# Sequence transform of batches 2 to 7: four 32-row tiles in two rounds, in place of two 63-row tiles in one stretch

## Chip, core and metric

The kernel runs on one core of a Trainium2 chip. The metric is the device time of one execution in microseconds (us); the time of a kernel is the median of its runs.

## What is computed

```python
X = np.fft.fft(x, axis=1)          # x: 8 batches x 3008 points x 256 features, f32
X = np.fft.fft(X, axis=2).real     # only the real part is kept
t = X.reshape(24064, 256)
gate = 1 / (1 + np.exp(-(t @ w_gate)))     # w_gate, w_val: 256 x 1536
out = (gate * (t @ w_val)) @ w_out         # w_out: 1536 x 256
```

## The kernel before

The transform along the features is multiplied into the gate and value weights once, at the start (`merge`, L331 and L332). What is left for each batch is a cosine and a sine transform along the 3008 points, and the gated network on its results.

**Steps.** The main loop has 576 steps, 72 for each batch (`per`): six chunks of 252 (the last 246) frequencies times twelve 128-wide tiles of the 1536 hidden features. Step i issues on TensorE (PE), in this order: `front_a` (two products into PSUM tile `pf`, from `pk`, the cosine transform), `back` (five products of hidden tiles `h` and their sums `sf` with the output weights `wf`, into the five PSUM banks `po0` to `po4`, for hidden tiles that are five steps older), and `front_b` (two products into `pf` from `qk`, the sine transform). Every f32 product is two weight loads and two matmuls in the trace. ScalarE (ACT) takes, in each step, a sigmoid (L658), a doubled copy of `pf` (`part`, L644), two writes that start the `pf` of the next step (`seed`, L629) and a second sigmoid (L672). `front_b(i)` adds into `pf` and so waits for `part(i)`. VectorE (DVE) takes three gate operations per step (L659, L671, L675; L675 waits for the second sigmoid), and two or three from the list `later` (sums and transposes of finished chunks, L765 and L773). GpSimd (POOL) forms the sums `sf` (L681), seven in one step of three and six in another; `back` reads them in the third to fifth step after.

**Transform of the next batch.** During the 72 steps of one batch the next one is prepared. DMAs on SyncE's queue (SP) write a mirrored copy of its input into DRAM (`mirror_x`, L157 to L166) and load it (`load_x`, L147) into the one buffer `x4`. POOL folds it there in 24 operations (`fold_ops`, L405 to L443), DVE adds six turns (`turn`, L454). At step 40 of the 72, right behind `front_b`, `whole` runs the four groups (block 0 or 1; cosine or sine) in one stretch on PE: per group 12 products of 63 or 62 rows, even rows of the input into PSUM tile `ev` with partitions 0 to 63, odd rows into `od` with partitions 64 to 127, each with 189 or 188 columns of the tables in tile `st`. ACT copies (L512, L518) and 16 DVE operations (L514, L524, L528) put them together into the `pk` and `qk` of the next batch. The tables for batches 1 to 7 are made once, during batch 0 (`table_again`, `table_odd`, L212 to L225).

The order of all engines is written by hand: each engine executes its instructions in the order in which the program issues them. `at(i, f)` puts `f` at the end of step i:

```python
def at(i, *fs):
    side.setdefault(i, []).extend(fs)
```

Of the kernel before, what the change touches and what calls it, by code (L numbers as in the profile page):

```python
# [12 lines left out]
ALU = mybir.AluOpType  # L13
# [68 lines left out]
def kernel(  # L82
# [50 lines left out]
    def mm(o, l, r, start, stop):  # L133
        nc.tensor.matmul(o, l, r, start=start, stop=stop, skip_group_check=True)  # L134
# [13 lines left out]

    XR = {}

    def mirror_x(b):


        copy = nc.sync.dma_start
        src = xf[b]
        dst = XR[b] = dram.tile([P, 4, NQ, D], F32, name=f"xr{b}")
        ops = [lambda: copy(out=dst[HP - 2 : HP, :, NQ - 1],  # L157
                            in_=zero[:, :, 0:D].to_broadcast([2, 4, D]))]

        def rows(par):  # L160
            copy(out=dst[par * HP : (par + 1) * HP, :, 0:N3], in_=src[0:HP, :, par:NQ:2])

        def mirror(par, q):
            t = M // 2 - 2 * q - par
            lo, p0, n = par * HP, t // NQ, HP - 2 * ((par, q) == (0, N3 - 1))
            copy(out=dst[lo : lo + n, :, N3 + q].rearrange("p h d -> h p d"),  # L166
                 in_=src[p0 - n + 1 : p0 + 1, :, t % NQ].rearrange("p h d -> h p d")[:, ::-1])
        for par in range(2):
            ops.append(lambda par=par: rows(par))
            ops += [lambda par=par, q=q: mirror(par, q) for q in range(N3)]  # L170
        return ops
# [59 lines left out]
        return tangent, lambda: inner(0), lambda: half(0), lambda: inner(1), lambda: half(1), ends  # L231

    assert NPR == 6
    jobs = [(0, 0), (1, 0), (0, 1), (1, 1), (2, 0), (0, 2), (1, 2), (2, 1), (0, 3), (1, 3), (0, 4), (1, 4),
# [157 lines left out]

    W = {}
    TURN = {}

    def fold_ops(b, nq):
        x4 = X.pop(b)
        if not b:  # L400
            x4 = x4[0:NP]
        ops = []

        def point(e, i, j, q):
            e.tensor_tensor(x4[:, i, q, 1:D], x4[:, i, q, 1:D], x4[:, j, q, D - 1 : 0 : -1],  # L405
                            op=ALU.add)

        def first(e, i, j, q):
            e.tensor_tensor(x4[:, i, q, 0], x4[:, i, q, 0], x4[:, j, q, 0], op=ALU.add)

        def feat(e, v, r, q):
            e.memset(r[:, q, 0:1], 0.0)
            e.tensor_tensor(r[:, q, 1:HD], v[:, q, 1:HD], v[:, q, D - 1 : HD : -1],
                            op=ALU.subtract)
            e.tensor_tensor(v[:, q, 1:HD], v[:, q, 1:HD], v[:, q, D - 1 : HD : -1], op=ALU.add)

        def across(e, blk, q):
            e.tensor_tensor(x4[:, 1 - blk, q], x4[:, 0, q], x4[:, 2, q],  # L418
                            op=(ALU.add, ALU.subtract)[blk])

        parts = [(x4[:, 1], x4[:, 3]), (x4[:, 0], x4[:, 2])]
        qs = [slice(q, q + nq) for q in range(0, NQ, nq)]
        pool = nc.gpsimd
        if b == 1:

            for i in (0, 2):
                ops.append(lambda i=i: first(pool, i, i + 1, slice(0, NQ)))
            for q in qs:
                ops += [lambda i=i, q=q: point(pool, i, i + 1, q) for i in (0, 2)]
            for q in qs:  # L430
                ops += [lambda blk=blk, q=q, e=pool if q is qs[-1] else nc.vector: across(e, blk, q) for blk in range(2)]
        elif b:

            for i in (0, 2):
                ops += [lambda i=i, q=q: point(pool, i, i + 1, q) for q in qs]
                ops.append(lambda i=i: first(pool, i, i + 1, slice(0, NQ)))
            for blk in range(2):
                ops += [lambda blk=blk, q=q: across(pool, blk, q) for q in qs]
        if b:
            ops += [lambda q=q: feat(pool, *parts[1], q) for q in qs]  # L440
            for i, op in enumerate((ALU.add, ALU.subtract)):
                for ds in (slice(0, HD), slice(HD, D)):
                    ops.append(lambda i=i, op=op, ds=ds: pool.tensor_tensor(  # L443
                        x4[:, 3, i * N3 : (i + 1) * N3, ds], x4[:, 1, 0:N3, ds],
                        x4[:, 1, N3:, ds], op=op))
            parts[0] = x4[:, 3], x4[:, 1]
            slots = x4.rearrange("p i q d -> p (i q) d")

            def turn(q, minus):

                y = [slots[:, q : q + 16 : 15], slots[:, q + N3 : q + N3 + 10 : 9]]
                if minus:
                    y.reverse()
                nc.vector.scalar_tensor_tensor(  # L454
                    out=y[0][:, :, HD:D], in0=y[1][:, :, 0:HD], scalar=(ST[3], ST[4])[minus][:, q : q + 1],
                    in1=y[0][:, :, 0:HD], op0=ALU.mult, op1=ALU.add)
            TURN[b] = [lambda q=q, minus=minus: turn(q, minus) for q in range(N3) for minus in range(2)]
            ops += [lambda q=q: feat(pool, *parts[0], q) for q in qs]
        else:

            def half_rows(q):
                even, odd = slice(0, 4, 2), slice(1, 4, 2)
                point(nc.vector, even, odd, q)
                first(nc.vector, even, odd, q)
                for blk in range(2):
                    across(nc.vector, blk, q)
                v, r = x4[:, 0:2, q], x4[:, 2:4, q]
                for to, op in ((r, ALU.subtract), (v, ALU.add)):
                    nc.vector.tensor_tensor(to[:, :, :, 1:HD], v[:, :, :, 1:HD], v[:, :, :, D - 1 : HD : -1],  # L469
                                            op=op)  # L470
                nc.vector.memset(r[:, :, :, 0:1], 0.0)
            ops += [lambda q=q: half_rows(q) for q in qs]
        for blk, (v, r) in enumerate(parts):
            if b and blk:
                W[b, blk] = v[:, :, HD:D], r[:, :, HD:D]
                continue
            W[b, blk] = v[:, :, 0:HD], r[:, :, 0:HD], v[:, :, HD : HD + 1]
        return ops
# [52 lines left out]
    def whole(b, blk, what):  # L531
        _, then, both = seq_group(b, blk, what, (2, 3) if what else (0, 1))
        both()
        return then()

    def seq_start(b):
        PQE[b] = [pqp.tile([P, NK + 1], F32, name=name, tag=name) for name in ("pk", "qk")]
# [331 lines left out]
    e_rows(0)  # L869

    per = NFT * len(chunks)
    side = {}

    def at(i, *fs):
        side.setdefault(i, []).extend(fs)
# [34 lines left out]
    for i in range(i0, count, i0):  # L910
        at(i - (8 if i == i0 else 11), lambda i=i: e_rows(i))

    for b in range(B - 1):
        s0 = b * per
        g0 = s0 + 3 * i0 + 4 if b else 5 * i0 + 4


        slots = [i for i in range(s0 - 2 * i0 if b > 1 else s0 if b else 2 * i0, g0 - 2)
                 if i % i0 < (4 if b > 1 else 6)]

        def folds(slots, b=b):
            ops = fold_ops(b + 1, 2)
            for i, f in enumerate(ops):
                at(slots[i * len(slots) // len(ops)], f)
            for i, f in enumerate(TURN.pop(b + 1)):
                at(58 + i if b == 0 else slots[-1] - 1 + i * 4 // 6, f)
        if b == 0:

            slots = [20, 20, 20, 21, 21, 22, 23, 24, 24, 25, 26, 27, 27, 29, 31, 33, 35, 37, 39, 41, 43, 50, 53, 55]
            assert len(slots) == 24  # L930
        at(slots[0] - 1, lambda slots=slots, folds=folds: folds(slots))
        at(g0 - 2, lambda b=b: seq_start(b + 1))
        for blk in (1, 0):
            at(g0, *[lambda b=b, blk=blk, what=what: whole(b + 1, blk, what)() for what in range(2)])
        if b < B - 2:
            at(g0 + 1, lambda b=b: load_x(b + 2))
            for i, f in zip(calm(s0 if b else 3 * i0), mirror_x(b + 2)):
                at(i, f)

    at((B - 2) * per + 4 * i0 + 8, lambda: [at((B - 2) * per + 4 * i0 + 9 + 2 * i, f) for i, f in enumerate(plain_ops())])  # L940

    for i in range(count):
        if i != 1:
            front_a(i)
        if i == 0:
            front_a(1)
        if i:
            gate_a(i - 1)
        part(i)
        if i == 0:  # L950
            weight_parts(5)
        if N1 <= i + 1 < count:
            seed(i + 1)
        if i:
            gate_b(i - 1, *join.pop(i, []))
        for f in pre.pop(i, []) + out_use.pop(i, []):
            f()
        if i >= 5:
            back((i - 5) // 3, (i - 5) % 3)
        merges = use.pop(i, [])  # L960
        for f in merges[0 : min(i, 1)]:
            f()
        front_b(i)
        for f in merges[min(i, 1) :]:
            f()
        n = 3 if i >= count - 8 else 2 + (i % 2 and i not in (3 * i0 + 7, 3 * i0 + 9))
        for f in later[0:n]:
            f()
        del later[0:n]
        for f in side.pop(i, []):  # L970
            f()
# [55 lines left out]
```

## Time and profile before

| | |
|---|---|
| runs | 1923.06, 1923.21, 1923.45 us; median 1923.21 |
| span of the profiled execution, from first to last instruction | 1921.4 us; its whole time is not shown apart, the runs' median is 1.8 us more than the span |
| granted TensorE clock | 1.000 |
| busy: PE / DVE / ACT / POOL | 99% / 74% / 70% / 79% |
| one step in the steady state | 3.125 us of PE, from one `front_a` to the next |
| steps 78, 83 and 84 begin at | 305.1, 320.7 and 323.9 us |
| steps 113 and 125 begin at | 423.0 and 460.6 us |

How to read it: a line of a table of groups gives the source line, the engine, the operation, what it writes and reads with shapes and count, then busy time and the mean of one, then the engine's idle time just before them and who ended it. A timeline row gives start and length; rows of the same instruction are merged ("x2"). "63*128" is rows times columns of the weights of a matmul.

### The profile page before, as it was taken

To read this page: it belongs to the slowest core of one execution; us is meant where nothing else is said; L and a number is where in the kernel's file an instruction comes from. 1 tells how busy PE (TensorE), PEld (TensorE's weight loads), DVE (VectorE), ACT (ScalarE), POOL (GpSimd) and SP (SyncE) were. 2 spreads that over 40 slices of the span, in tenths; PEclk is the share of its full clock that TensorE was granted. 3 is DMA by queue.
4 is the path that set the end of the run, shared out by engine and by line. 5 is a ranking of instruction groups with operands and counts; after the bars stand their busy time and mean duration, and the time that the engine had idled before them with its cause. 6 is when DMAs were issued, how large, how long until landed. Compare 5 with 4: busy or idle time off the path is not lost.

```text
span 1921.4 us, 34211 instructions
## 1 busy us (share of the span) xinstructions
PE 1910.5 (99%) x11164; PEld 1776.2 (92%) x11164; DVE 1429.4 (74%) x3225; ACT 1344.2 (70%) x3148; POOL 1524.8 (79%) x2733
## 2 busy tenths in 40 slices
PE   8999999999999999999999999999999999999999
PEld 5789999999999999999999999999999999999998
DVE  7677877787777777778677777777777687777775
ACT  4876767767777677776777767777677767777775
POOL 2489969978898788987888878888788977877770
PEclk9999999999999999999999999999999999999999
DMA  8353222120131211202111121121200100011011
GB/s 313 110 98 78 66 80 60 48 80 15 22 78 23 80 20 41 61 14 82 26 47 48 20 84 19 47 52 23 80 15 15 27 15 15 14 21 21 15 16 31
DMA packets 173633, 97.02 MB, mean 50 GB/s; under 512 B 134429, under 2 KB 164360, under 8 KB 171664
## 3 DMA queue, kind: packets, MB, share of 16 engines
q1 hardware_dynamic: 172878, 94.32, 20.2%
q8 instruction: 90, 1.47, 0.3%
q14 instruction: 87, 0.71, 0.1%
q10 hardware_dynamic: 546, 0.51, 0.1%
q0 software_dynamic: 32, 0.00, 0.0%
HBM read 70.08 MB, written 46.71 MB: 61 GB/s over the span
## 4 chain that ended last, share of the span: by engine, by line
PE 98%; DMA 1%; DVE 1%; ACT 0%; issue 0%; SPq 0%; ACTq 0%
PE pf L134 51%; PE po L134 43%; PE ev L134 3%; DMA x<-in_xf_dram 1%; PE od L134 1%; PE ps L134 1%; DMA raw<-in_moe_w_val_dram 0%; PE pe L134 0%; DVE z L659 0%; DVE wf L307 0%; ACT wl L389 0%; DVE x L418 0%; DVE x L469 0%; DVE x L405 0%; ACT ae L644 0%
## 5 line engine op out<-in xcount | busy, mean ns | idle before, releaser
L681 POOL TENSOR_TENSOR sf<-h 128x168 f32<-128x168 f32 (+1 forms) x920 | 511.0, 575 | 215.5 <-DVE h L675 215.2
L681 POOL TENSOR_TENSOR sf<-h,sf 128x168 f32<-128x168 f32 (+1 forms) x1104 | 616.4, 579 | 56.5 <-DVE h L675 56.2
L134 PE MATMUL pf<-pk,G 128*128 128x252 f32 (+1 forms) x2304 | 582.7, 376 | 0.0
L134 PE MATMUL pf<-qk,G 128*128 128x252 f32 (+1 forms) x2304 | 582.1, 375 | 0.2 <-ACT ae L644 0.2
L675 DVE TENSOR_TENSOR h<-pf,z 128x252 f32<-128x252 f32 (+1 forms) x576 | 241.7, 420 | 418.5 <-ACT pf L672 418.5
L629 ACT ACTIVATE pf<-ek,ge 128x252 f32<-128x252 f32 (+1 forms) x1142 | 538.1, 471 | 20.4 <-DMA ge<-G 1.0
L134 PE MATMUL po<-sf,wf 128*128 128x168 f32 (+1 forms) x2944 | 508.2, 305 | 0.0
L644 ACT ACTIVATE ae<-pf 128x504 f32<-128x504 f32 (+1 forms) x576 | 339.7, 590 | 233.8 <-PE pf L134 232.5
L134 PEld LDWEIGHTS pf<-pk,G 128*128 128x128 f32 x2304 | 436.7, 190 | 52.6 <-issue 2.3
L134 PEld LDWEIGHTS po<-sf,wf 128*128 128x128 f32 x2944 | 453.4, 190 | 8.0
L134 PE MATMUL po<-h,wf 128*128 128x168 f32 (+2 forms) x2584 | 459.6, 306 | 0.0
L134 PEld LDWEIGHTS pf<-qk,G 128*128 128x128 f32 x2304 | 411.0, 190 | 30.4 <-issue 1.8
L765 DVE TENSOR_TENSOR c<-c 128x168 f32<-128x168 f32 (+1 forms) x920 | 430.5, 500 | 4.8
L134 PEld LDWEIGHTS po<-h,wf 128*128 128x128 f32 x2584 | 411.4, 190 | 17.0 <-issue 0.9
L659 DVE TENSOR_TENSOR z<-ae,pf 128x504 f32<-128x504 f32 (+1 forms) x576 | 383.7, 666 | 33.2 <-ACT h L658 31.7
L658 ACT ACTIVATE h<-pf 128x252 f32<-128x252 f32 (+1 forms) x576 | 218.2, 379 | 163.5 <-PE pf L134 159.4
L672 ACT ACTIVATE pf<-z 128x252 f32<-128x252 f32 (+1 forms) x576 | 214.2, 372 | 79.5 <-DVE h L671 76.6
L671 DVE TENSOR_TENSOR h<-h,pf 128x252 f32<-128x252 f32 (+1 forms) x576 | 233.0, 404 | 0.0
L681 POOL TENSOR_TENSOR sf<-sf 128x168 f32<-128x168 f32 (+1 forms) x184 | 106.0, 576 | 14.4
L681 POOL TENSOR_TENSOR sf<-sf,h 128x168 f32<-128x168 f32 (+1 forms) x184 | 100.7, 547 | 0.0
L748 ACT COPY c<-po 128x504 f32<-128x504 f32 (+1 forms) x138 | 78.5, 569 | 0.0
L773 DVE STREAM_TRANSPOSE os<-c 128x256 f32<-128x256 f32 x188 | 72.4, 422 | 0.4 <-issue 0.3
(139 smaller groups left out, 899.8 us busy)
## 6 DMA issues: line engine op xcount, KB each, us to landing
x<-xr SPq DMA_DIRECT2D x14, 1536.0 KB
out_dram<-os SPq DMA_DIRECT2D x368, 56.0 KB
xr<-in_xf_dram SPq DMA_DIRECT2D x14, 768.0 KB
xr<-in_xf_dram SPq DMA_DIRECT2D x35, 256.0 KB
ek<-ed SPq DMA_DIRECT2D x40, 126.0 KB
out_dram<-os SPq DMA_DIRECT2D x284, 7.0 KB
x<-in_xf_dram SPq DMA_DIRECT2D x3, 1024.0 KB
st<-in_stab_dram SPq DMA_DIRECT2D x3, 753.0 KB
```

The costliest lines, as they stand in the source:

```text
L134: nc.tensor.matmul(o, l, r, start=start, stop=stop, skip_group_check=True)
L629: nc.scalar.activation(PF[i][:, g], EK[i // NFT], AF.Copy, scale=ge[:, g, f : f + 1])
L644: nc.scalar.activation(AP[i], PF[i], AF.Copy, scale=2.0)
L658: nc.scalar.activation(H[p][:, fh, 0:n], PF[i][:, 0], AF.Sigmoid)
L659: nc.vector.tensor_tensor(z[:, :, ::-1], AP.pop(i), PF[i], op=ALU.subtract)
L671: nc.vector.tensor_tensor(h[:, fh, 0:n], h[:, fh, 0:n], pf[:, 1], op=ALU.mult)
L672: nc.scalar.activation(pf[:, 0], z[:, 0], AF.Sigmoid)
L675: nc.vector.tensor_tensor(h[:, fh, n:], pf[:, 0], z[:, 1], op=ALU.mult)
L681: nc.gpsimd.tensor_tensor(block(p, dst), block(p, a), block(p, b), op=(ALU.subtract, ALU.add)[op])
L748: (nc.vector.tensor_copy if t == 1 or t == 3 else nc.scalar.copy)(C[0][:, 3 * t * R : 3 * (t + 1) * R], PO[t][:, 0 : 3 * R])
L765: nc.vector.tensor_tensor(t[:, dst * R : (dst + 1) * R], *v, op=(ALU.subtract, ALU.add)[op])
L773: nc.vector.transpose(os_[0][:, s, 0:nb, h, :], t[:, c0 : c0 + nb * TB])
```

## The change

Batches 2 to 7 are folded once more, so that the same frequencies come from four tiles of 32 rows (`TILES`), each with 95 columns, in place of two of 63 rows with 189. Batch 1 keeps the old form.

- Tables: during batch 1 (steps 73 to 84) the table tile is filled again. Six DRAM copies and 16 loads, 16 sums of 32 rows on POOL (`four`, `eight`), two multiplications on ACT (`halves`) and some 20 operations on three to six columns, most on DVE, make it.
- The mirrored copy has 23 DMAs per batch in place of 9 (`quarter_x`). The load into `x4` stands at step 54 of the 72, before at step 41. The first 17 folds on POOL stand in the first five steps of the chunks from step -12 to 16, the last seven at steps 24 to 37; before, the 24 were spread over steps -24 to 38.
- Two sets of eight DMAs (`swap`, steps 24 and 39) copy features between the row groups inside `x4`, and 15 DVE operations (`more`) add the copies.
- `quarter` runs block 1 at step 41 and block 0 at step 53, between `front_a` and `back`: 48 products each, into banks `po1` to `po4`, and eight ACT copies of 190 columns each. `back` of the step before stands ahead of its `gate_b`. Twenty DVE operations at steps 54 to 73 put the parts together (`quarter_ends`).
- `gate_b` takes one DVE operation between its two products in every step: a turn, a `more`, one of `quarter_ends`, or else the first of `later`, of which one less follows at the end of the step.

The core of the diff (`st`, `j4`, `r4`, `ev` and `odd` are parts of the table tile; `i0` is 12):

```diff
+    TILES = [(g, par, par * HP + g * TB) for g in range(2) for par in range(2)]
...
+        def clear():
+            pool.memset(j4, 0.0)
+            pool.memset(r4, 0.0)
+            pool.memset(ev[:, :, :, NE:], 0.0)
+
+        def four(t, which):
+            for g, par, lo in TILES:
+                if par != which:
+                    continue
+                at_, e = rows(lo), (g + t) % 2
+                m = slice(1 - e, last)
+                pool.tensor_tensor(j4[at_, t, :, m], odd[at_, t, :, 4 - 2 * e : NO : 4],
+                                   odd[at_, t, :, 3 - 2 * e : NO - 1 : 4], op=ALU.add)
+
+        def eight(g, which):
+            for _, par, lo in TILES[2 * g : 2 * g + 2]:
+                at_ = rows(lo)
+                for t in range(2):
+                    if par == which:
+                        pool.tensor_tensor(r4[at_, t, :, 1:last], ev[at_, t, :, 5 : NE - 2 : 4],
+                                           ev[at_, t, :, 3 : NE - 4 : 4], op=(ALU.add, ALU.subtract)[g])
+
+        def halves():
+            nc.scalar.mul(j4, j4, 0.5)
+            nc.scalar.mul(r4, r4, 0.5)
...
+            def swap(blk):
+
+                hs, here, there = (((1, 3), slice(0, HD), slice(HD, D)), ((0, 2), slice(HD, D), slice(0, HD)))[blk]
+                for g, par, lo in TILES:
+                    o = lo + (TB, -TB)[g]
+                    for h in hs:
+                        nc.sync.dma_start(out=x4[lo : lo + TB, h, :, there], in_=x4[o : o + TB, h, :, here])
+
+            def more(v, blk, c, q):
+
+                here, there = ((slice(0, HD), slice(HD, D)), (slice(HD, D), slice(0, HD)))[blk]
+                here, there = (v[..., ds] for ds in (here, there))
+                nc.vector.scalar_tensor_tensor(out=here, in0=there, scalar=c[:, q : q + 1], in1=here,
+                                               op0=ALU.mult, op1=ALU.add)
+            MORE[b] = ([lambda: swap(0), lambda: swap(1)],
+                       [lambda q=q, a=a: more(slots[:, 9 + q : 19 + q : 9] if a == 0 else slots[:, (0, 21, 6)[a] + q],
+                                              0, TAB[("other", "cx", "cy")[a]], q)
+                        for q in range(N3) for a in range(3)],
+                       [lambda q=q, a=a: more(slots[:, q + N3 : q + N3 + 10 : 9] if a else slots[:, q : q + 16 : 15],
+                                              1, TAB["other"][:, N3:], q) for q in range(N3) for a in range(2)])
...
+    def quarter(b, blk):
+
+        ps = [bank("sum", t + 1) for t in range(4)]
+        for what in range(2):
+            for part in range(2):
+                for q in range(N3):
+                    for t, (g, par, lo) in enumerate(TILES):
+                        rows = slice(lo, lo + TB - ((par, q) in ((0, 2), (1, 1), (1, 2))))
+                        if blk:
+                            w, tab = q + N3 * part, TAB["j4"][rows, what ^ part, q]
+                        elif part:
+                            w, tab = q + N3 * (1 - what), TAB["r4"][rows, what, q]
+                        else:
+                            e = 2 * ((g + what) % 2)
+                            w, tab = q + N3 * what, TAB["ev"][rows, what, q, e : e + 4 * NQ4 - 3 : 4]
+                        c0 = (2 * what + 1 - part) * NQ4
+                        mm(ps[t][:, c0 : c0 + NQ4], W[b, blk][what][rows, w], tab,
+                           what == part == q == 0, q == N3 - 1)
+        for t, (g, par, lo) in enumerate(TILES):
+            for what in range(2):
+                e = (g + what) % 2
+                oy = 1 - e if blk else g
+                to = TAB["at"] + 2 * NQ4 * (4 * (2 * blk + what) + par) + oy
+                pitch = 4 * NQ4 + e - oy
+                to = TAB["full"][:, to : to + 2 * pitch].rearrange("p (x k) -> p x k", x=2)[:, :, 0 : 2 * NQ4 - 1 : 2]
+                nc.scalar.copy(to, ps[t][:, 2 * what * NQ4 : 2 * (what + 1) * NQ4].rearrange("p (x k) -> p x k", x=2))
...
-    for b in range(B - 1):
-        slots = [i for i in range(s0 - 2 * i0 if b > 1 else s0 if b else 2 * i0, g0 - 2)
-                 if i % i0 < (4 if b > 1 else 6)]
...
-        for blk in (1, 0):
-            at(g0, *[lambda b=b, blk=blk, what=what: whole(b + 1, blk, what)() for what in range(2)])
-        if b < B - 2:
-            at(g0 + 1, lambda b=b: load_x(b + 2))
-            for i, f in zip(calm(s0 if b else 3 * i0), mirror_x(b + 2)):
...
+    at(per + 1, quarter_tables)
+    for i in range(4):
+        at(per + 2 + i, lambda i=i: quarter_load(i // 2, i % 2))
+
+    def make_tables():
+        small, large = quarter_ops()
+        for i, f in zip((6, 7, 9, 10, 11, 12), small):
+            at(per + i, f)
+        for i, f in enumerate(large):
+            at(per + 7 + i // 2, f)
+    at(per + 5, make_tables)
+
+    def later_folds(b, s0):
+
+        ops = fold_ops(b, 2)
+        slots = [i for i in range(s0 - (3 if b == 2 else i0), s0 + i0 + 5) if i % i0 < 5 or i < s0 and b == 2]
+        for i, f in enumerate(ops[0:17]):
+            at(slots[i * len(slots) // 17], f)
+        for i, f in zip((24, 25, 26, 27, 28, 36, 37), ops[17:], strict=True):
+            at(s0 + i, f)
+        for i, f in enumerate(TURN.pop(b)):
+            gap[s0 + 18 + i] = [f]
+        swaps, last, first = MORE.pop(b)
+        at(s0 + 24, swaps[1])
+        at(s0 + 39, swaps[0])
+        for i, f in enumerate(first):
+            gap[s0 + 28 + i] = [f]
+        for i, f in enumerate(last):
+            gap[s0 + 43 + i] = [f]
+
+    def later_ends(b, s0):
+        one, two = quarter_ends(b, 1), quarter_ends(b, 0)
+        for i, f in enumerate(one[0] + two[0] + one[1] + two[1]):
+            gap[s0 + 4 * i0 + 6 + i] = [f]
+
+    for b in range(2, B):
+        s0 = (b - 1) * per
+        at(s0 - 4 if b == 2 else s0 - i0 - 1, lambda b=b, s0=s0: later_folds(b, s0))
+        at(s0 + 3 * i0 + 2, lambda b=b: seq_start(b))
+        for blk in range(2):
+            mid[s0 + (4 - blk) * i0 + 5] = lambda b=b, blk=blk: quarter(b, blk)
+        at(s0 + 4 * i0 + 5, lambda b=b, s0=s0: later_ends(b, s0))
+        if b < B - 1:
+            at(s0 + 4 * i0 + 6, lambda b=b: load_x(b + 1))
+            for i, f in enumerate(mirror_x(b + 1)):
+                at(list(calm(s0))[i // 2], f)
...
+        if i + 1 in mid:
+            back((i - 5) // 3, (i - 5) % 3)
+        n = 3 if i >= count - 8 else 2 + (i % 2 and i not in (3 * i0 + 7, 3 * i0 + 9))
+        between = gap.pop(i, [])
+        if not between and later and i < count - 8:
+            between = [later.pop(0)]
+            n -= 1
         if i:
-            gate_b(i - 1, *join.pop(i, []))
+            gate_b(i - 1, *join.pop(i, []), *between)
+        del between
         for f in pre.pop(i, []) + out_use.pop(i, []):
             f()
-        if i >= 5:
+        mid.get(i, lambda: None)()
+        if i >= 5 and i + 1 not in mid:
             back((i - 5) // 3, (i - 5) % 3)
```

## The prediction

> **What bounds the kernel now.** I read the page first, its busy times and its chain of work:
>
> ```profile
> PE 1910.5 (99%) x11164; PEld 1776.2 (92%) x11164; DVE 1429.4 (74%) x3225; ACT 1344.2 (70%) x3148; POOL 1524.8 (79%) x2733
> ...
> PEclk9999999999999999999999999999999999999999
> ...
> PE 98%; DMA 1%; DVE 1%; ACT 0%; issue 0%; SPq 0%; ACTq 0%
> PE pf L134 51%; PE po L134 43%; PE ev L134 3%; DMA x<-in_xf_dram 1%; PE od L134 1%; PE ps L134 1%; DMA raw<-in_moe_w_val_dram 0%; PE pe L134 0%; DVE z L659 0%; DVE wf L307 0%; ACT wl L389 0%; DVE x L418 0%; DVE x L469 0%; DVE x L405 0%; ACT ae L644 0%
> ```
>
> TensorE sets the end, at full clock; in the steady state each step takes 3.125 us of it without a gap. So a gain has to be PE time, and a loss is whatever makes PE wait. The transform is the 4% under `ev` and `od`. The timeline of PE where batch 2 is transformed, with its ends:
>
> ```profile
> 413.74 1.01 PE L134 MATMUL pf<-qk,G 128*128 128x252 f32 x4
> 414.69 0.42 PE L134 MATMUL ev<-st,x 63*128 63x189 f32 x1
> 414.69 0.42 PE L134 MATMUL od<-st,x 63*128 63x189 f32 x1
> 414.95 0.32 PE L134 MATMUL ev<-st,x 63*128 63x189 f32 x1
> 414.95 0.32 PE L134 MATMUL od<-st,x 63*128 63x189 f32 x1
> 415.11 0.32 PE L134 MATMUL ev<-st,x 63*128 63x189 f32 x1
> 415.12 0.32 PE L134 MATMUL od<-st,x 63*128 63x189 f32 x1
> ...
> 422.59 0.49 PE L134 MATMUL od<-st,x 62*128 62x188 f32 x2
> 423.01 0.91 PE L134 MATMUL pf<-pk,G 128*128 128x252 f32 x3
> ```
>
> The two row groups start together, every 0.16 us; from the first `ev` to the next `pf` are 8.32 us, and nobody was waited for. Six such stretches (49.9 us) are what the change replaces. The weight loads there:
>
> ```profile
> 414.68 0.18 PEld L134 LDWEIGHTS ev<-st,x 63*128 63x128 f32 x1 [0.33 <-issue]
> 414.69 0.18 PEld L134 LDWEIGHTS od<-st,x 63*128 63x128 f32 x1
> 414.79 0.19 PEld L134 LDWEIGHTS ev<-st,x 63*128 63x128 f32 x1
> ```
>
> The two groups load side by side, and a group's second load follows its first by 0.108 us: that is the least that 128 columns of weights take.
>
> **The rounds.** A matmul of n columns follows the last by n x 0.833 + 2.5 ns (252: 212.5; 168: 142.5 apart), so 95 columns would take 82 ns; the weights, 108, come last. I take 109 ns for a set of four tiles. Going in and out of row groups costs 0.39 us (the first and second starts are 94 and 99 ns late against 212 and 159, the two at the end 96 and 104). A round is 24 sets: 24 x 0.109 + 0.39 = 3.0 us, two are 6.0, a gain of 2.3 per batch and **13.9 us** for six. That four tiles run at once is shown by `pe` (four column tiles of 377 columns: 16 records in 1.46 us from 179.41, where one after another would need 16 x 0.316 = 5.1). Bounds: 82 ns a set gives 4.7 us for the two and 21.6 for six batches; for the other end see (d).
>
> A round needs `po1` to `po4` empty. The last bank's copy (L748, 570 ns) starts at the latest 1.6 us after `front_a` of the step before ends, where `back` takes 1.43, `front_b` and `front_a` then 1.70: covered by about 0.9 us. Behind a round `back` fills `po0` for 0.86 us before it needs `po1`, whose two ACT copies take 0.32 each (L512) after the last matmul's end: I add 0.1 us a round for the hand-over, 1.2 us in all (0 to 4). The eight copies, 2.6 us, lie where ACT waits for `front_b` anyway (2.27 us after the round).
>
> **Work that PE does not see.** DVE loses 16 operations per batch (8 x 0.35 + 8 x 0.55 = 7.2 us) and gets 15 `more` and 20 ends (17.6, from 0.715 for 256 elements, 0.55 for 376, 0.35 for 188). They stand in the gap before L675:
>
> ```profile
> L675 DVE TENSOR_TENSOR h<-pf,z 128x252 f32<-128x252 f32 (+1 forms) x576 | 241.7, 420 | 418.5 <-ACT pf L672 418.5
> ```
>
> The last column but one is idle time: 0.73 us each time, as long as the longest of the new operations. So 10.4 us per batch cost nothing; without that gap they would come on top of 74% busy, still under PE. For SP it is 30 DMAs more per batch of 0.35 to 0.65 us: 18 of 233 us, in a queue that waited 1221 us for `os`. The swaps (8 DMAs, about 4 us of issue, some 3 us to land) are behind stores that end near step 25.3, so they land near step 27.6, wanted at 28.7. The load of `x4` moves 3.1 MB in 10 us (268 and 361 GB/s in two windows from 423, then 0); it has six steps, 18.7 us. All at 0; if a swap were late, DVE would stand in front of L675 with it, some us per batch. The POOL folds per step rise from about 4.4 to 5.7 per chunk; a running sum puts the sums `sf` 1.3 to 1.8 us late, of over 6 us that they have.
>
> **The tables of batch 2** are the one place with a price. I add up POOL's queue from consecutive starts: `sf` 0.53 (one of three steps 7, another 6), folds 1.25 (510 and 512 elements). The nine folds from step 69 leave POOL at 11.1 us after the start of step 78, where 6.8 is usual. Then, up to the end of its work of step 83: `sf` 20 x 0.53 = 10.6; two clears of 570 elements 1.4 (252 took 0.34); and 16 sums of 280 elements and 32 rows, 0.76 each on a line through 168, 254, 512. Not one has a row of its own. One after the other they are 12.2 us. The nearest row for fewer partitions:
>
> ```profile
> 220.71 0.30 POOL L219 COPY st<-st 128x3 f32<-128x3 f32 x1
> 220.94 0.10 POOL L220 MEMSET st<- 128x3 f32 x1
> 220.98 0.18 POOL L224 COPY st<-st 64x3 f32<-64x3 f32 x1
> 221.11 0.10 POOL L225 MEMSET st<- 64x3 f32 x1
> ```
>
> The next instruction starts 0.23 us after a copy of 128 rows and 0.13 after one of 64. I take it that rows out of use let the next one begin: every row group then has 4 sums and passes 12 at 0.1, 4.2 us. POOL is done 11.1 + 10.6 + 1.4 + 4.2 = 27.3 us after step 78 begins, 8.5 after step 84 does (6 x 3.125 = 18.75). For this the second `halves` waits on ACT at the end of step 83, and behind it in ACT's queue stand the sigmoid and `part(84)`, for which `front_b(84)` waits on PE. In the trace `part(84)` starts 1.05 after the step and `front_b` at 2.28; then it is 8.5 + 0.66 + 0.38 + 0.59 + 0.1 = 10.2. PE stands **8.0 us**, once. Bounds: 2.4 (POOL not behind, sums for nothing; the wait stands behind seven `sf` all the same) to 16 (one after the other).
>
> The Trainium skill (GPSIMD Engine Reference, 2.1 Instruction dispatch) says that each of the eight cores serves 16 partitions and starts the next instruction when its own share is done. The trace agrees as far as 0.23 against 0.13 go. By it the wait is the 8 us, without it 16.
>
> **Sum**, against the profiled execution: 1921.4 - 13.9 + 1.2 + 8.0 = 1916.7 of span; with the 1.8 us that the runs' median has more, **1918.5 us**.
>
> **Rivals.**
> (a) POOL's small sums run one after the other: 8 us more, 1926.5. For it: the two halves' copies are 0.26 apart in start, which does not show an overlap. Against it: 0.13.
> (b) The block is short, 2.4 to 5 us, because POOL is less late or the sums are cheap: 1913 to 1915. For it: 32 rows have no row here.
> (c) Reading every fourth f32 of `ev` (block 0, 12 of the 48 sets of a batch) streams at half rate: 158 in place of 109 ns, 6 x 12 x 0.049 = 3.5 us, 1922. For it: pairs with every second element read (and written) took 168, those without 159. The Trainium skill (SBUF — State Buffer, Door 1: The DMA port swizzle) says that a 16-byte line needs two hits for full bandwidth, and a step of four f32 has one; the trace has no such step.
> (d) Slower: four tiles can't be fed. A set has eight records. No row shows PE starting records faster than one per 79 ns on average (both the `ev` pairs and `pe` are at 79, which their columns explain as well). At 40 ns a record a set takes 160, a round 4.2, the twelve 50.8 in place of 49.9: 1923.2 + 0.9 + 1.2 + 8.0 = 1933. From 125 ns a set on, nothing is gained. Against it: eight weight loads of `pe` started within 0.06 us.
> (e) The change does not do what it says: POOL, DVE or SP hold PE in each batch, as with a late swap; 1 us a batch gives 1924.5.
>
> **How the numbers follow.** Forecast 0.45 (by itself 1914 to 1922); (a) 0.12; (b) 0.17; (c) 0.08; (d) 0.10; (e) 0.08. About 0.2%, 3.8 us, is what a measurement of this kernel can tell from no change: 1919.4 to 1927.1 is the same. Faster: 0.35 of the forecast's and (b), 0.52. Same: 0.10, (a), (c), 0.30. Slower: (d), (e) in its larger sizes, 0.18. The range 1911 to 1929 leaves out the best of (b) with the low bound of the rounds, and (d) with the worst of (e).
>
> **What would show it.** In the profile after: rounds of `sum` of 3.0 us with four starts together every 0.109 us, twelve of them (0.16 for (d); slower in block 0 than in block 1 for (c)); one wait of ACT for POOL of some 6 us around 326 us (`halves`), PE idle there and nowhere else; L675's idle time down; POOL rows of 32 rows (their starts decide (a)). Wrong would be PE waits that come back with every batch, or a gap on PE around 326 us that is missing.

## The result and the profile after

The changed kernel takes 1936.11 us (median of four runs, 1935.79 to 1936.39), the kernel before beside it 1923.13. The ratio is 1.0068 (95% interval 1.0055 to 1.0080): 13.0 us slower, where 1918.5 was forecast with a range from 1911 to 1929. The span of the profiled execution is 1934.6 us against 1921.4, 13.2 us longer.

The page of the changed kernel, the lines that answer to those of before (busy times, granted clock, chain by engine):

```profile
PE 1908.1 (99%) x11740; PEld 1767.9 (91%) x11740; DVE 1517.2 (78%) x3359; ACT 1351.3 (70%) x3214; POOL 1554.7 (80%) x2760
...
PEclk9999998899999999999999999999999999999999
...
PE 96%; DMA 2%; POOL 1%; DVE 1%; ACT 1%; SPq 0%; issue 0%; ACTq 0%; DVEq 0%; POOLq 0%
```

PE's busy time is only 2.4 us less, although six stretches became shorter, and the clock row has two 8s in its seventh and eighth slices (290 to 387 us), where it was 9 throughout. DMA and POOL now have 2% and 1% of the chain. So something happened once, early, and it also cost PE its clock.

To place it I took the start of every step (its first `front_a`) from both traces and subtracted the lengths. All differences add up to 13.3 us:

| steps | before to after, us | forecast, us |
|---|---|---|
| 78 to 82 | +10.25 | 0 |
| 83 to 86 | +11.67 | +8.0 |
| six stretches of `whole` removed | -50.53 (8.42 each) | -49.9 |
| six first rounds (block 1) | +17.74 (2.96 each) | +18.6 with hand-over |
| six second rounds (block 0) | +22.36 (3.73 each) | +18.6 with hand-over |
| tenths elsewhere | +1.8 | 0 |

The gain of the transform is there, 10.4 us. Two waits take back 21.9. The waits of the changed kernel from 305 to 350 us (engine, line, releaser; us in total, times, longest):

```profile
PE pf L134 <- ACT ae L882: 16.7, 2, 9.2
ACT pf L910 <- DVE h L909: 12.9, 5, 9.3
ACT st L375 <- POOL st L370: 8.6, 1, 8.6
DVE z L897 <- ACT h L896: 7.9, 2, 7.3
DVE st L317 <- DMA st<-in_stab_dram: 7.0, 1, 7.0
```

Read it from the bottom. DVE waits 7.0 us, at the second instruction of `turns`, for a table load; behind it in DVE's queue stand the gates, so ACT waits 9.3 us for a gate (L909), and PE for ACT's `part` (L882). That is the first stop. The second begins on ACT: the second `halves` (L375) waits 8.6 us for POOL's last table sum, DVE waits 7.3 us for the sigmoid behind it, and PE 9.2 us. PE's line names ACT both times, and ACT is the cause in neither. SP's queue shows why the load is late:

```profile
312.37 0.62 SPq L169 DMA_DIRECT2D xr<-in_xf_dram  x1
313.03 0.60 SPq L304 DMA_DIRECT2D st<-in_stab_dram  x1
313.68 0.43 SPq L304 DMA_DIRECT2D st<-rtab  x1
```

The loads are put at steps 74 to 77, which end by 304.5 us, but SP issues stores, the 16 loads and the copies for batch 3 one after another, and comes to the last odd tables at 313.03 and 313.68. `turns` reads all odd tables, and its second operation starts at 318.18.

What a stop costs beyond its length, in windows around the first one (after the window's length: busy time with instruction count of PE, PEld, DVE, ACT, POOL; then the granted clock, the DMA share, GB/s):

```profile
313.00:314.00 1.00, 0.20 (x2) 0.00 (x0) 0.00 (x0) 0.00 (x0) 1.00 (x3) 1.00 0.62 121
315.00:316.00 1.00, 0.00 (x0) 0.00 (x0) 0.00 (x0) 0.00 (x0) 0.92 (x3) 0.77 0.99 314
320.00:321.00 1.00, 0.30 (x1) 0.30 (x2) 1.00 (x3) 1.00 (x3) 0.92 (x2) 0.50 0.27 96
325.00:326.00 1.00, 1.00 (x6) 1.00 (x6) 0.00 (x0) 0.97 (x4) 1.00 (x3) 0.61 0.26 84
326.00:327.00 1.00, 1.00 (x8) 0.95 (x7) 0.74 (x2) 0.23 (x1) 0.92 (x2) 1.00 0.09 28
```

PE ends at 313.2. In the third microsecond behind that the granted clock falls to 0.50, and it is still 0.50 when PE goes on at 320.7; it is back at about 325.8 (0.61 over that microsecond is 0.22 us at full clock). So PE works 5.1 us at half speed and loses 2.5 us more: 7.5 standing + 2.5 = 10.0 of the 10.25. In the second stop PE stands 9.2 us and then works 4.5 us at half speed: 9.2 + 2.3 = 11.5 of the 11.67. The Trainium skill (TensorE: Matmul & The Clock Gate, What's actually happening) has the clock halved after an idle window of about 3.4 us, in windows that run freely, and full again after a busy one. The trace agrees as to the windows: the clock was half for 10.24 us both times, three times 3.41. But it was halved 2.3 us after PE's end here and 3.5 us in the second stop, so the window ahead of the first halving was not idle throughout: PE still worked in its first 1.1 us.

The rounds (start, length, "x96" is the 24 sets of four tiles; first a round of block 1, then one of block 0):

```profile
436.76 2.93 PE L134 MATMUL sum<-st,x 32*128 32x95 f32 x96
```
```profile
477.32 3.60 PE L134 MATMUL sum<-st,x 32*128 32x95 f32 x96
```

In the first, four matmuls start within 20 ns of each other, a set every 111.5 ns. In the second, the 12 sets that read every fourth element of `ev` are 170 ns apart, the 12 that read `r4` are 112: 12 x 0.058 = 0.70 us.

### The profile page after: what moved, and what is told of

Same layout as the page of the kernel before. It is cut to its first block, busy times and chain, and to the rows that moved or that the text cites. A ratio compares the mean times of both kernels' runs of the same rounds, so it can differ in the third digit from the quotient of the medians.

```text
span 1934.6 us, 35834 instructions
## 1 busy us (share of the span) xinstructions
PE 1908.1 (99%) x11740; PEld 1767.9 (91%) x11740; DVE 1517.2 (78%) x3359; ACT 1351.3 (70%) x3214; POOL 1554.7 (80%) x2760
## 4 chain that ended last, share of the span: by engine, by line
PE 96%; DMA 2%; POOL 1%; DVE 1%; ACT 1%; SPq 0%; issue 0%; ACTq 0%; DVEq 0%; POOLq 0%
PE pf L134 50%; PE po L134 42%; PE sum L134 2%; DMA x<-in_xf_dram 1%; PE ps L134 1%; PE ev L134 1%; POOL sf L919 0%; DMA raw<-in_moe_w_val_dram 0%; DMA st<-in_stab_dram 0%; POOL st L370 0%; PE od L134 0%; DMA st<-rtab 0%; POOL st L362 0%; SPq L304 0%; DVE z L897 0%
## 5 line engine op out<-in xcount | busy, mean ns | idle before, releaser
L919 POOL TENSOR_TENSOR sf<-h 128x168 f32<-128x168 f32 (+1 forms) x920 | 520.6, 585 | 172.3 <-DVE h L913 170.2
L882 ACT ACTIVATE ae<-pf 128x504 f32<-128x504 f32 (+1 forms) x576 | 339.4, 589 | 220.8 <-PE pf L134 219.1
L913 DVE TENSOR_TENSOR h<-pf,z 128x252 f32<-128x252 f32 (+1 forms) x576 | 240.8, 418 | 283.1 <-ACT pf L910 279.9
L134 PEld LDWEIGHTS pf<-qk,G 128*128 128x128 f32 x2304 | 411.4, 190 | 48.9 <-ACT ae L882 17.9
L1003 DVE TENSOR_TENSOR c<-c 128x168 f32<-128x168 f32 (+1 forms) x920 | 448.9, 510 | 3.2
L909 DVE TENSOR_TENSOR h<-h,pf 128x252 f32<-128x252 f32 (+1 forms) x576 | 233.3, 405 | 0.0
L919 POOL TENSOR_TENSOR sf<-sf 128x168 f32<-128x168 f32 (+1 forms) x184 | 101.6, 552 | 14.4
L919 POOL TENSOR_TENSOR sf<-sf,h 128x168 f32<-128x168 f32 (+1 forms) x184 | 108.6, 590 | 0.0
L1011 DVE STREAM_TRANSPOSE os<-c 128x256 f32<-128x256 f32 x188 | 77.3, 429 | 0.4 <-issue 0.3
```

What stands on the lines that cost most here:

```text
L882: nc.scalar.activation(AP[i], PF[i], AF.Copy, scale=2.0)
L909: nc.vector.tensor_tensor(h[:, fh, 0:n], h[:, fh, 0:n], pf[:, 1], op=ALU.mult)
L913: nc.vector.tensor_tensor(h[:, fh, n:], pf[:, 0], z[:, 1], op=ALU.mult)
L919: nc.gpsimd.tensor_tensor(block(p, dst), block(p, a), block(p, b), op=(ALU.subtract, ALU.add)[op])
L1003: nc.vector.tensor_tensor(t[:, dst * R : (dst + 1) * R], *v, op=(ALU.subtract, ALU.add)[op])
L1011: nc.vector.transpose(os_[0][:, s, 0:nb, h, :], t[:, c0 : c0 + nb * TB])
```

## The experiments

Theory at this point: the loss is two queues around the tables of batch 2 (a load late in SP's queue in front of DVE's gates; POOL's sums in front of ACT's sigmoid), and the stride of `ev` takes 4 us of the gain. Rival: the two waits are one, POOL being overloaded, and mending a wait only moves it. Ratios are to the kernel before on the same chip, 1923 us, with 95% intervals. The columns of steps are differences to it as in the table above.

| kernel | us | ratio | steps 78-82 | 83-86 | 87-111 |
|---|---|---|---|---|---|
| changed kernel | 1936.11 | 1.0068 (1.0055 to 1.0080) | +10.25 | +11.67 | -0.1 |
| e1_turns_late | 1935.83 | 1.0066 (1.0052 to 1.0079) | 0 | +19.17 | +2.4 |
| e2_sums_spread | 1935.88 | 1.0066 (1.0053 to 1.0078) | +10.18 | +0.83 | +10.9 |
| e3_both | 1924.03 | 1.0005 (0.9996 to 1.0014) | +1.4 | 0 | +8.0 |
| e5_no_sums | 1918.31 | 0.9977 (0.9968 to 0.9986) | 0 | 0 | +4.3 |
| e6_odd_first | 1932.63 | 1.0051 (1.0038 to 1.0065) | +1.2 | +16.4 | -0.1 |
| e8_best | 1917.37 | 0.9971 (0.9961 to 0.9982) | 0 | +0.2 | +6.9 |
| e9_spread | 1912.55 | 0.9945 (0.9932 to 0.9959) | 0 | 0 | +2.1 |

### The two waits, one at a time and together

```diff
-        for i, f in zip((6, 7, 9, 10, 11, 12), small):
+        for i, f in zip((12, 13, 21, 22, 23, 24), small):
```

> The six small VectorE steps on the tables of batch 2 (turns, pairs, ratios, two crosses, minus) move from steps 78 to 84 to steps 84 to 96, nothing else; so VectorE no longer stands in front of the gate of step 79 with a table load that lands at 318.2 us. In the changed kernel PE lost 10.3 us there (7.5 standing, the rest at half clock) and 11.7 at step 84. Theory A, the two waits are links of one queue: POOL works through its folds, sums sf and table sums without a pause that PE's stop would cause, and ends the table sums some 2 us earlier at most (it idled 1.95 and 3.2 us, the first of them after the stop); the first wait goes and the second grows by some 8 us: 1934 us. Theory B, the waits are two prices that add: 1936.1 - 10.3 = 1925.8.

Measured: 1935.83 us. Theory A. The first stop is gone and the second grew from 11.67 to 19.17. ACT's and PE's waits from 305 to 350 us:

```profile
PE pf L134 <- ACT ae L882: 13.6, 1, 13.6
ACT st L374 <- POOL st L362: 9.1, 1, 9.1
ACT st L375 <- POOL st L370: 8.4, 1, 8.4
```

Now the first `halves` waits as well. While PE had stood at step 80, POOL had worked on and caught up; without that stop it is late by all of its work.

```diff
-        for i, f in enumerate(large):
-            at(per + 7 + i // 2, f)
+        for i, f in zip((10, 17, 18, 19, 20, 21, 22, 23, 32, 34, 35, 36), large, strict=True):
+            at(per + i, f)
```

> POOL's work on the tables (clears, the 16 sums of 32 rows, end columns) and ScalarE's halves move from steps 79 to 84 to steps 82, 89 to 95 and 104 to 108, where POOL has no folds; nothing else. The VectorE wait at step 79 stays. Theory (POOL's queue is what halves waited for): the 11.7 us at step 84 go and nothing takes their place, since 1.45 us of sums a step fit in the 1.35 us that POOL has free and the six us that sf is ahead: 1936.1 - 11.7 = 1924.4. Rival (POOL's work is too much wherever it stands): the wait comes back at PE as a wait for sf or at a later step, 1928 to 1936.

Measured: 1935.88 us. The theory fell and the rival holds: of the 11.67 us at steps 83 to 86, 0.83 stayed and 10.9 came back at steps 87 to 111, mostly at steps 96 and 107. At each of these two PE stood 2.3 us (at step 96 for `sf`), and its granted clock was 0.50 for 3.41 us from 0.3 to 0.4 us after it went on. In the waits of this kernel from 305 to 350 us stands

```profile
POOL sf L919 <- DVE h L913: 11.5, 6, 4.5
```

against 5.2 in the changed kernel: in the first stop (4.5 us) and in the steps behind it POOL ran out of gates to sum, with its table work not yet due, and had to do that work later, when it had no time.

> Both moves together. If the 13 us that the change lost are the two waits less what the rounds give back (six batches by 1.4 to 1.7 us), then 1936.1 - 10.3 - 11.7 = 1914.1, under the kernel before by 9 us. If the waits come back elsewhere, 1920 to 1936.

Measured: 1924.03 us. The moves that gain nothing singly gain 12 together, as two links in a row do; but 9.4 us stay, at steps 78, 79, 95 to 97, 102 to 107.

### What the last 9 us are

From `e3_both`, without the sums of 32 rows (`pass` in place of the two `pool.tensor_tensor`).

> The kernel with both moves (e3_both, 1924.0 us), without the 16 sums of 32 rows on POOL, so that the tables j4 and r4 hold no sums and the outputs of batches 2 to 7 are wrong. e3_both still lost 9.4 us between steps 78 and 107, where POOL was busy 98% of the time. Theory (POOL has no room: 16 x 0.70 = 11.2 us of sums against 6.4 us that it was idle from 300 to 420 us in the kernel before): without the sums the losses at steps 95 to 107 go, 8 us: 1916. Rival (VectorE's small steps on the tables, which stand together at the ends of steps 93 to 96, hold the gates): the 3.8 us of steps 95 to 97 stay: 1920.

Measured: 1918.31 us, between the two. Of the 9.4 us, 3.7 went with POOL's sums, at steps 87 to 111, and 4.3 stayed: 0.7 at step 107 and 3.7 at steps 95 to 97, where `ratios` and `cross` stand together at the ends of steps, the rival's share.

The other 1.4 us, at steps 78 and 79, are gone too, but not for lack of the sums, the first of which stands at step 89. In `e3_both` an addition of two operands on DVE, just ahead of step 78, found POOL at work without a pause:

```profile
301.98 2.42 DVE L1003 TENSOR_TENSOR c<-c 128x164 f32<-128x164 f32 x1
```

POOL's five sums `sf` ended at 304.21, the DVE operation 0.19 us later. In the changed kernel it took 0.41 us; in `e7_step_end` below, the same program up to step 90, it took 2.40 and steps 78 and 79 lost the same 1.4. So these 1.4 us come and go from one execution to the next.

That POOL's small sums do not overlap can be read in the changed kernel directly (rows of one form merged):

```profile
326.43 2.98 POOL L362 TENSOR_TENSOR st<-st 32x279 f32<-32x279 f32 x4
```
```profile
334.46 4.19 POOL L370 TENSOR_TENSOR st<-st 32x279 f32<-32x279 f32 x6
```

0.75 and 0.70 us from one to the next, none waiting for another engine, though neighbours use different rows (L362 each, L370 every second one): 32 rows cost about what the forecast's line gives for 128 rows of this length, 0.76. The sums read every fourth element and the rows of that line elements side by side; no run tells the two effects apart.

### The load, by its place in the queue

```diff
-    def quarter_load(t, par):
+    def quarter_load(t, part):
-        for name, cols in (("odd", slice(NE, NE + NO)), ("ev", slice(0, NE))):
-            for g, own, lo in TILES:
-                if own == par:
+        for name, cols in ((("odd", slice(NE, NE + NO)), ("ev", slice(0, NE)))[part],):
+            for g, par, lo in TILES:
+                if 1:
```

(The calls change with it: all odd tables at steps 74 and 75, all even ones at 76 and 77.)

> The changed kernel with its 16 table loads in another order: the eight of the odd columns, which the turns of step 78 read, ahead of the eight of the even ones; nothing else. In the changed kernel the last odd one is issued at 313.7 us and lands at 318.2. Theory (the wait is for the place of that load in SP's queue and for 2.26 MB that come at 215 GB/s): the odd loads are issued by 307 and landed by 309 to 312, so VectorE's wait of 1.65 + 7.0 us shrinks to 0 to 3; the time falls by little, to 1934 to 1936, since POOL's queue then holds step 84 longer, as when the turns were moved. Rival (the wait is for all loads of the tile, in whatever order): it stays at 7 us or more.

Measured: 1932.63 us, 1.4 below the expected range. DVE's waits from 305 to 350 us:

```profile
DVE st L327 <- DMA st<-st: 6.3, 1, 6.3
...
DVE st L317 <- DMA st<-rtab: 1.4, 1, 1.4
```

`turns` waits 1.4 and not 7.0 us, so the wait was the load's place. At once the next one is late: `ratios` (L327) waits 6.3 us for `pairs`' own transfer, which stands behind the same queue, and after it ACT waits 6.5 us for POOL's sums.

### The stride

```diff
-                            w, tab = ..., TAB["ev"][rows, what, q, e : e + 4 * NQ4 - 3 : 4]
+                            w, tab = ..., TAB["ev"][rows, what, q, 0:NQ4]
```

> The changed kernel, but the 12 sets of block 0 that read every fourth element of ev read as many elements that lie side by side (other columns of the table, so the sums of block 0 are wrong); sizes and counts are the same. In the trace of the changed kernel these sets are 170 ns apart and the others 112. Theory (the stride sets the pace): 12 x 0.058 = 0.70 us a batch, six batches 4.2 us: 1931.9, and second rounds as long as first ones. Rival (something else in block 0, such as the weights W of the halves): 1936.1.

Measured: 1932.06 us, ratio 1.0047 (1.0035 to 1.0060), and each second round 0.67 us shorter:

```profile
477.08 2.93 PE L134 MATMUL sum<-st,x 32*128 32x95 f32 x96
```

> The changed kernel, but the 12 sets of block 0 read every second element of ev and not every fourth (other columns, so the sums of block 0 are wrong). Read from the trace, by the pitch of these sets: every fourth took 170 ns, side by side 112 (the weights). Theory (four elements of f32 make a line, and a read gets its full rate while it uses two of a line): 112 ns, second rounds as long as first ones. Rival (any stride halves the rate): 158 to 170.

Measured, in a single run (1931.78 us; `0 : 2 * NQ4 - 1 : 2` in the same place):

```profile
477.00 2.93 PE L134 MATMUL sum<-st,x 32*128 32x95 f32 x96
```

Under the 112 ns that the weights take, a step of two elements costs nothing here; a step of four makes 95 columns take 170 ns. The Trainium skill (SBUF — State Buffer, Door 1: The DMA port swizzle) says that a read needs two hits in each 16-byte line, four f32, for full bandwidth; both kernels agree with it, though the weights would hide a small cost of the step of two (189 columns, read and written with that step, took 168 against 159 ns in the kernel before).

### Alone between gate products

The four `gap[...] = [f]` become `at(..., f)`: the 41 added DVE operations of a batch stand at the end of their steps.

> The changed kernel with its added VectorE operations (6 turns, 15 more, 20 ends a batch) at the end of their steps, ahead of the next sigmoid's product, and not alone between two gate products. Theory A (the place matters: there VectorE idles 0.73 us, at the step's end only 0.16): each of the 41 holds the gates by some 0.3 us, of which TensorE sees a part; 1940 to 1960. Theory B (VectorE has 0.7 us to spare in each step, wherever the work stands, and TensorE needs the gates only steps later): 1936, within 2 us.

Measured: 1942.61 us, ratio 1.0104 (1.0090 to 1.0118), 6.5 us over the changed kernel: theory A, near its lower end. Outside the two stops and the rounds the difference to the kernel before is 8.3 us where the changed kernel has 1.8. Of these 6.5 us, 5.0 stand at two steps of five batches, 139 and 143 and their like (0.66 and 0.34 us); for the last batch nothing is lost there. So the place is worth 6.5 us, but not 0.3 us for each of the 41: nearly all of it is lost where DVE's queue is full. From step 139 to the end of 143 DVE is busy 15.8 of 16.6 us, and its 22% of idle time over the whole is no cover there.

### The version that the runs point to

From the changed kernel: the eight sums of `j4` singly on DVE, the eight of `r4` as two operations of 128 rows (`scalar_tensor_tensor` with a sign per row), each in a gap before L913 of its own; `ev`'s columns copied once side by side by ACT.

```diff
-        for i, f in enumerate(large):
-            at(per + 7 + i // 2, f)
+        for i, f in zip((7, 8, 11, 12, 13, 14, 15, 16, 17, 24, 25, 26), sums, strict=True):
+            gap[per + i] = [f]
...
-                            w, tab = ..., TAB["ev"][rows, what, q, e : e + 4 * NQ4 - 3 : 4]
+                            w, tab = ..., TAB["e4"][rows, what, q]
```

> The changed kernel with the tables of batch 2 made on VectorE in place of POOL, one operation in a gap between gate products (two clears and eight sums of 32 rows at steps 79 to 90 and 96, and the other eight sums as two operations of 128 rows with a sign per row at steps 97 and 98), the small VectorE steps at steps 83 to 89, and every fourth column of ev copied once by ScalarE so that block 0 reads columns that lie side by side. If the losses of the change are POOL's queue, the late load and the stride, then 1936.1 - 22.0 - 4.1 = 1910.0. If VectorE's work holds the gates in their place, 1914 to 1922.

Measured: 1917.37 us, faster than the kernel before, 7.4 short of the theory: 5.8 us at steps 86 to 91, 1.4 at 101 to 108. There DVE's small steps stand in a row at a step's end. Their timeline, with the POOL operation beside them:

```profile
332.98 0.17 DVE L343 RECIPROCAL st<-st 32x3 f32<-32x3 f32 x1
333.19 1.01 DVE L344 TENSOR_TENSOR st<-st 32x3 f32<-32x3 f32 x1
```
```profile
331.69 2.50 POOL L584 TENSOR_TENSOR x<-x 128x512 f32<-128x512 f32 x2
```

Three elements a row take 1.01 us and end at 334.20, 0.02 us after POOL's fold (331.69 + 2.50 = 334.19, rounded); the reciprocal, with one operand, takes 0.17. The same product takes 0.23 and 0.28 us one step later. The Trainium skill (SBUF — State Buffer, SBUF: two separate sides) says that a DVE operation with two operands in SBUF and a POOL operation that reads SBUF exclude each other for a whole instruction; the end 0.02 us behind POOL's agrees.

> The version with the tables made on VectorE (e8_best, 1917.4 us), with its small VectorE steps taken apart and put one or two to a gap between gate products (the turns at steps 87 to 89, the ratios at 97 and 98, the crosses at 108 to 113, which nothing reads before step 115), and the sums, halves and ends of r4, which block 0 needs only at step 125, moved from steps 97 to 100 to steps 106 to 109. e8_best still lost 5.7 us at steps 86 to 91, where three to five small steps stand together at a step's end. Theory (place, not amount: the same work costs nothing when it stands singly in the gap): 1917.4 - 5.7 = 1911.7. Rival (each VectorE operation with two operands in SBUF waits for POOL's, wherever it stands): 1915 to 1917.

Measured: 1912.55 us, ratio 0.9945 (0.9932 to 0.9959): 10.5 us faster than the kernel before, 23.6 faster than the changed kernel, with the same fold, its tables made elsewhere and `ev` read side by side. The theory holds but for 0.9 us: the 5.8 us at steps 86 to 91 became 1.3, and the 1.4 at 101 to 108, where the sums of `r4` moved as well, 0.2. In all 2.1 us are still lost before step 112. Its windows there show how full it is:

```profile
320.00:340.00 20.00, 20.00 (x116) 18.79 (x115) 19.59 (x37) 14.56 (x34) 19.84 (x30) 1.00 0.42 96
340.00:360.00 20.00, 19.24 (x108) 17.16 (x108) 19.85 (x40) 11.71 (x28) 19.61 (x37) 1.00 0.14 49
```

DVE is busy 19.6 to 19.9 of 20 us (13.5 and 17.2 in the kernel before), POOL 19.6 to 19.8, and PE stands for 0.8 us only.

## Why the prediction was wrong

It missed by 17.6 us, 17.9 in the span. By the steps: first stop 10.2, second 3.7, rounds and stretch 2.3 (10.4 gained, 12.7 forecast), tenths elsewhere 1.8.

**The step that failed: "All at 0", and "PE idle there and nowhere else".** In "the one place with a price", the tables, only POOL's queue was priced. The swaps of `x4` were followed through SP's queue, behind the stores, to the microsecond at which they are wanted. The 16 table loads go through the same queue and were not followed. The same reckoning would have pointed at it: 16 issues behind the stores, 2.26 MB that take 6 to 8 us even at the 268 to 361 GB/s read for `x4` (10.5 at the 215 seen here), first issued at 303.4, and wanted at 309.4, when DVE comes to `turns`. By these it gives up to 2.4 us, and 4.5 at 215 GB/s; the 8.6 seen came with the copies for batch 3 that stand among the loads. That the wait sits on DVE in front of the gates made it PE's. The rule for an added wait, who is queued behind it, was applied to `halves` on ACT only. The range held no such term, and with rival (e)'s "in each batch" none of the rivals was a single stop in this place.

**The second stop: right in its place, wrong in its parts.** `halves` waited for POOL at step 84, as forecast, and PE stood 9.2 us against 8.0. But the 16 sums were priced at 4.2 us, overlapping by row groups, and take 11 to 12 us one after the other: rival (a). The two errors hid each other, since POOL caught up during the first stop, so 9.2 against 8.0 is luck. With that stop gone (`e1_turns_late`), PE lost 19.2 us: 13.6 and 2.9 standing and, by the granted clock, 2.0 at half speed (the other 0.7 is not traced). Rival (a)'s 16 comes near the standing part, but 2.9 of that was a wait for `sf`, which no case had. The Trainium skill (GPSIMD Engine Reference, 2.1 Instruction dispatch) was read as a price for rows out of use; these rows show no such gain, whatever the reason, and 0.23 against 0.13 us for three elements was too thin a row to carry it.

**The clock.** No term of the sum had it: 2.5 and 2.3 us for the two stops, 4.8 in all, since all stalls were priced by their length.

**The rounds.** The pitch, 109 ns, was 111.5, and the first round with its hand-over 2.96 against 3.1; that four tiles of weights can be fed is shown, rival (d) is out. (Its sum was wrong as well: eight records at 40 ns are 320 ns and not 160.) The second round is rival (c): 170 ns where 158 was priced, 4.0 us in all where 3.5 was, and it holds together with the others, while the forecast gave the time of one case alone.

**Work that PE does not see.** DVE's idle time before L913 fell from 418.5 us to

```profile
L913 DVE TENSOR_TENSOR h<-pf,z 128x252 f32<-128x252 f32 (+1 forms) x576 | 240.8, 418 | 283.1 <-ACT pf L910 279.9
```

so the gap took the added operations in as forecast, but for the tenths: 1.6 of the 1.8 us stand at steps 139 to 142 and their like (0.3 us for each of five batches), where DVE is busy 12.28 of 12.50 us (10.04 of 12.20 in the kernel before). And `e7_step_end` shows that without it they cost 6.5 us more; the forecast had them "still under PE" in that case, which was wrong. The load of `x4` and the swaps held nothing back: behind step 125 no step of the changed kernel is over 0.2 us longer than before, the rounds apart.

What stays open: no run shows that DVE's full queue makes these tenths, why POOL's small sums do not overlap, or whether the fold can start the tables earlier than step 73, where their tile comes free.

## What to carry to other kernels

Follow every transfer that somebody waits for through its queue, once-only ones too, and ask what is queued behind the waiting instruction; one instruction that waits on an engine which feeds the bottleneck costs nearly as much as if the bottleneck itself had waited (8.6 us on DVE were 7.5 on PE), and a stop of some microseconds can cost PE its clock on top (2.3 us did twice in `e2_sums_spread`, and did not in `e3_both`). When several late queues stand in a row, mending one shows nothing: here two moves were worth 0 and 0 singly and 12 us together, so test them together before giving up either. A slot where an engine idles each time is worth more than its mean idle time: the same small steps cost up to 2.2 us a step in a row at a step's end, and at most 0.7 taken apart in the gap.

## What the runs showed of the hardware

- Four row tiles of 32 rows with 128 columns of weights start together every 111.5 ns, with 95 columns streamed side by side or, in the one run with it, at a step of two f32; at a step of four 170 ns.
- TensorE's granted clock fell to 0.50 at 2.3 and 3.5 us after its last matmul, and was full again 5.1 and 4.5 us after the next. In `e1_turns_late`, after 2.9 us idle, 1.1 busy and idle again, it fell 0.5 us after the last. In `e2_sums_spread` two stops of 2.3 us were enough; the half clock began 0.3 to 0.4 us after PE had gone on. In `e3_both` a stop of 2.3 us left it full. The half clock lasted 3.41 us in `e2_sums_spread` and 10.24 in each stop of the changed kernel.
- POOL's sums of 279 elements that read every fourth element take 0.70 to 0.75 us on 32 rows, one after the other, also when the rows differ.
- A DVE product of 32x3 elements took 0.23 to 1.01 us in one kernel; the 1.01 ended 0.02 us behind a POOL fold. An addition of 128x164 took 0.41 us or, beside five sums of POOL without a pause, 2.42.
